# Threshold attention and a SoLU layer on one core: turning the weights of four slots on TensorE, and earlier loads

## The chip, the core and the metric

The kernel runs on one core of a Trainium2 chip. The metric is the device time of one execution in microseconds; before the change it is 865.18 us, the median of three runs (863.53 to 865.64). The engines are TensorE (PE, with its weight loads PEld), VectorE (DVE), ScalarE (ACT), GpSimd (POOL) and the queue engine SyncE (SP), which issues most of the transfers. Each works through its own list of instructions in order and waits on semaphores of the others.

## What is computed

Eight batches, eight heads, 576 rows of 64 per head: attention in which only scores within tau of the row's largest count, then a layer on the 4608 rows of 512 that result.

```python
scores = scale * np.matmul(q, k.transpose(0, 1, 3, 2))
thresh = np.max(scores, axis=-1, keepdims=True) - tau
scores = np.where(scores >= thresh, scores, -1000000000.0)
attn = np.exp(scores - np.max(scores, axis=-1, keepdims=True))
attn = attn / (np.sum(attn, axis=-1, keepdims=True) + 1e-09)
x = np.matmul(attn, v)                  # (B,H,S,D) -> rows of H*D = 512
h = x @ w_in                            # 512 x 1024
sm = softmax(h); solu = h * sm
ln = (solu - mu) / np.sqrt(var + 1e-06) * g_ln
out = ln @ w_out                        # 1024 x 512
```

All is float32; the two weight matrices and g_ln arrive as 64-bit numbers and are turned into float32 on the chip.

## The kernel before

**Slots and rounds.** The attention is cut into 144 slots, 18 to a batch. A slot is 128 score rows (64 rows twice) of a pair of heads, `(b, kind, hp, r)`: batch, half of the sequence, pair of heads, and first or second 128 rows. Slots 0 to 7 are the first half of batch 0, two for each of four pairs of heads. The main loop has a round for each slot, and the order of each engine's instructions is the order in which the loop writes them. In round s:

- `scores` (L472): TensorE multiplies q and k of slot s into two PSUM tiles `s_ps`, one per head, 576 columns each. If k and q of a later pair have to be turned, those products (L337) come first, into spare columns of the same tiles, and `keeps` copies them out (L374, L399, L415, L419).
- `maxes` (L494): VectorE reduces both tiles to the row's extreme and adds tau.
- `ramp` (L509) and `exps` (L518): ScalarE makes the threshold and the exponential, with the row's sum.
- `normalise(s - 1)` (L525 to L528): POOL inverts the sums of the slot before and scales its weights `w`, 576 columns for each head.
- `blocks(s - 1)` (L540, L549, L551): VectorE transposes them in 32 x 32 blocks into `T`; after the second slot of a pair SP issues three transfers that reorder the blocks into `wT`, 1.18 MB in all.
- `attend_steps` (L582) and `attended` (L614): three or four rounds after the pair's second slot TensorE multiplies v by `wT`, in 36 products of 128 columns (72 records in the trace), into a PSUM tile `pv`, and ScalarE copies the result to `xh`. The list `pv_due` holds the rounds: 5, 7, 9 and 10 for the pairs of slots 0 to 7.

**The layer.** When four pairs are in, `xh` holds two tiles of 128 rows. For each tile TensorE computes h in two rounds (`ff_h`, L647), then VectorE, ScalarE and POOL make maximum, exponential, product, statistics and normalisation (`ff_max` L662 to `ff_norm2` L718), a transfer swaps halves (`ff_swap` L729), VectorE transposes (`ff_turn` L739), and TensorE computes the output in two rounds (`ff_o`, L752). The first h stands in round 11, then 12, and 13 and 14 for the second tile; the first output stands in round 17.

**Weights.** The sixteen pieces of the two matrices are handled one a round in rounds 0 to 15: loaded four rounds ahead (`weight_load`, L270), taken apart by VectorE (L284, L287, L302) and ScalarE (L290), added by POOL (L312). The pieces of w_out are also multiplied by g_ln (L317) and copied to the other half of the partitions by two transfers (`weight_d`, L324). An output product may not start before the sixteenth piece.

**PSUM.** Four tiles of two banks: `s0` and `s1` for the scores, `p0` and `p1` (handed out by `take`) for everything else: turned heads, `pv`, `h_ps`, `o_ps`.

**Buffers.** `w` has four buffers (two slots), `wT` two, `u` and `V`, which the layer uses, one each.

**Loads.** `load_at` gives the round in which SP issues a load: v of batch 0 in rounds 0, 1, 3 and 5; k and q of batch 1 in rounds 10, 11, 15 and 16; its v in 17, 18, 24 and 25. SP issues in order too, and a transfer that waits for a buffer holds back those behind it.

Of the kernel before, what the change touches and what calls it, by code (L numbers as in the profile page):

```python
# [20 lines left out]
def kernel(  # L21
# [47 lines left out]
    ident = const.tile([P, P], F32, name="ident")  # L69
    swapped = const.tile([P, 64], F32, name="swapped")  # L70
    w1 = const.tile([P, NP, DFF], F32, name="w1")
# [147 lines left out]
    def constants():  # L219

        nc.gpsimd.memset(seed, 0.0)
        nc.scalar.activation(out=ntau, in_=seed, func=AF.Exp)
        make_identity(nc, ident)
        for g in range(2):
            of = 64 + 32 * (1 - g)
            nc.gpsimd.tensor_copy(
                out=swapped[ROWS[1], 32 * g : 32 * g + 32], in_=ident[ROWS[1], of : of + 32]
            )
        nc.gpsimd.memset(mhalf, -0.5)
        nc.gpsimd.memset(mone, -1.0)  # L230
        nc.gpsimd.memset(zero, 0.0)

        nc.vector.tensor_scalar(
            out=scl, in0=tau_t, scalar1=0.0, scalar2=SCALE, op0=ALU.is_ge, op1=ALU.mult
        )
        nc.vector.tensor_scalar(
            out=tau_t, in0=tau_t, scalar1=0.0, scalar2=104.0, op0=ALU.max, op1=ALU.min
        )  # L240
        nc.vector.tensor_scalar(out=ntau, in0=tau_t, scalar1=-1.0, scalar2=None, op0=ALU.mult)
# [89 lines left out]
    def turn(spare, x, lhsT_of, swap=False):  # L331

        o = spare["base"] + 64 * x
        to = slice(o, o + 64)
        for r in range(2):
            for y in range(2):
                nc.tensor.matmul(  # L337
                    out=spare[r][ROWS[y], to], lhsT=lhsT_of(r, y),
                    rhs=swapped[ROWS[1]] if swap and r else ident[ROWS[r], ROWS[r]],
                    start=True, stop=True,  # L340
                )
# [106 lines left out]
    live = {}  # L448

    def scores(s, items):  # L450
        b, kind, hp, r = slots[s]
# [9 lines left out]
        for ks in (slice(SM, S), slice(0, SM)):  # L461
            for h in range(2):
                for y in range(2):
                    if kind < 2:
                        d = pairs[b * NP + hp]
                        t = P * (2 * kind + r) if b < 2 else 32 * NK * r + P * kind
                        t += 64 * y
                        lhsT = d["qT"][ROWS[h], t : t + 64]
                    else:
                        d = pairs[b * NP + r + 2 * y]  # L470
                        lhsT = d["qe"][ROWS[h]]
                    nc.tensor.matmul(  # L472
                        out=ps[h][ROWS[y], ks], lhsT=lhsT, rhs=d["kT"][ROWS[h], ks],
                        start=True, stop=True,
                    )
# [31 lines left out]
    def ramp(s, x):  # L507
        d = live[s]
        nc.scalar.activation(  # L509
            out=d["w"][x], in_=d["w"][x] if d["loose"] else d["ps"][x][:, 0:S], func=AF.Prelu, bias=d["nth"][x], scale=-1.0,  # L510
            alpha=1.0e30,
        )
# [9 lines left out]
    def normalise(s):  # L522
        d = live[s]
        sm = d["sm"]
        nc.gpsimd.tensor_scalar(out=sm, in0=sm, scalar1=1e-9, scalar2=None, op0=ALU.add)  # L525
        nc.gpsimd.tensor_tensor(out=sm, in0=sm, in1=mone, op=ALU.pow)  # L526
        for x, w in enumerate(d["w"]):
            nc.gpsimd.tensor_scalar(  # L528
# [29 lines left out]


    def attend_steps(key):  # L560
        b, kind, hp = key
        unit = units[key]
        wT = unit["wT"]
        unit["y"] = take("pv")
        _, y = unit["y"]
        y = y.rearrange("p (u n) -> p u n", u=2)

        for e in range(2) if kind == 2 else [None]:
            for m in range(NK):
                for u in range(2):  # L570
                    d, h0 = source(b * NP + (hp if e is None else e + 2 * u))
                    for h in range(2):
                        if e is None:
                            how = "p (r g x) -> p g r x" if b < 2 else "p (g r x) -> p g r x"
                            to = y[ROWS[h], u, 0:P].rearrange(how, r=2, g=2)
                            rhs = wT[ROWS[u], :, m, :, h]
                        else:
                            to = y[ROWS[h], u, 64 * e : 64 * e + 64].rearrange(
                                "p (g x) -> p g x", g=2
# [11 lines left out]
                        yield  # L591

    def attended(key):
        b, kind, hp = key
        tag, y = units.pop(key)["y"]
        y = y.rearrange("p (u n) -> p u n", u=2)[:, :, 0:P]
# [10 lines left out]
        else:  # L607
            if hp == 0:
                xh[b, kind] = work.tile(
                    [P, NP, 256], F32, tag=f"xh{(2 * b + kind) % 4}", bufs=1, name="xh"  # L610
                )
            how = "p (r u y) -> p u r y" if b < 2 else "p (u g x r) -> p u g r x"
# [185 lines left out]
    for s, (b, kind, hp, r) in enumerate(slots):  # L798
        if r == 1:
            pv_due.append((s + LAG_PV + (s < 6 or s in (11, PER - 1, PER + 9)), (b, kind, hp)))  # L800
# [17 lines left out]
    for at, job, hf, what in (  # L818
        (11, load_one, 0, "q"),
        (10, load_one, 0, "k"),  # L820
        (15, load_one, 1, "k"),
        (16, load_one, 1, "q"),
        (17, load_v, 0, (0,)),
        (18, load_v, 0, (1, 2)),
        (PER + 6, load_v, 1, (0,)),
# [34 lines left out]
    with tc.manual_schedule():  # L860
# [16 lines left out]
        whole = {0: 1, 2: 2, 4: 3}  # L877
        for r, hf, parts in ((0, 0, (0,)), (1, 0, (1, 2)), (3, 1, (0,)), (5, 1, (1, 2))):
            load_at[r] = [lambda hf=hf, parts=parts: load_v(0, hf, parts)]

        ready = []
# [8 lines left out]
        while True:  # L890
# [10 lines left out]
            if rnd == NS:  # L901
# [8 lines left out]
                assert quarter != 3  # L910
            if rnd == 13:
                prev, cur, quarter = cur, None, 0
# [9 lines left out]
            if more:  # L922
# [18 lines left out]
                maxes(rnd, loose)  # L941
                ramp(rnd, 0)
                if rnd == 0:
                    weight_a(0)
                if not loose:
                    keeps(rnd, 0)
                    keeps(rnd, 1)
                ramp(rnd, 1)
                exps(rnd)
            if rnd in whole:  # L950
# [30 lines left out]
            elif step == ("h", 1):  # L981
                ff_h(cur, 1, None, beside)
                quarter = 2
                by = rnd + 2 * (rnd == 14)
                late.setdefault(by, []).append(lambda t=cur: (ff_max(t), ff_exp(t)))
# [9 lines left out]
                if cur == (0, 1, 1):  # L995
                    middle.setdefault(rnd + 6, []).append(lambda t=cur, at=rnd + 6: ff_turn(t, at))
                else:
                    late.setdefault(at, []).append(lambda t=cur, at=at: ff_turn(t, at))
                if not more:
# [15 lines left out]
            if attending is not None:  # L1015
# [6 lines left out]
                elif kind < 2 and hp == NP - 1:  # L1022
                    ready.append((rnd + 1, [(b, kind, 0), (b, kind, 1)]))
            if rnd - 1 in live:
                blocks(rnd - 1)
# [8 lines left out]
            if rnd == 3:  # L1034
                gains()
            if rnd in pieces:
                x = pieces[rnd]
                weight_b(x)
                for y in {0: (3, 4), 11: (), 12: (15,)}.get(x, (x + 4,)):
                    if y < len(pieces):  # L1040
                        weight_load(y)
                if x + 1 < len(pieces):
                    weight_a(x + 1)
            for job in load_at.pop(rnd, []):
# [39 lines left out]
```

## Time and profile before

| | |
|---|---|
| median of three runs | 865.18 us |
| the profiled execution | 864.95 us, its span 863.2 us |
| PE busy | 817.0 us (95%) |
| VectorE, ScalarE, POOL busy | 673.5, 572.1, 495.1 us |
| PE idle before 118.4 us, and after | 34.9 us, 11.3 us |
| granted TensorE clock, mean | 0.981 |

The rounds begin (start of the first L494, in us) at 35.14 (round 5), 40.37, 44.33, 49.25, 53.51 (round 9), 60.34, 70.05 (round 11), 74.46, 80.88, 85.95, 92.47 (round 15), 100.24, 105.19, 110.20 (round 18) and 118.40 (round 19).

The busy time of an engine is read stage by stage, since the first 118 us, in which the weights are prepared, go by other limits than the rest. A line of waits gives the waiting engine with tile and line, the releaser, the sum in us, how often, and the longest. A line of the chain gives a start, a length in us and what ran; a line of the timeline adds count and, in brackets, the idle time before it and who ended it.

### The profile page before, as it was taken

Reading aid. Unit: us, or ns where it says so; the run is one execution under the profiler, and the core shown is the slowest. Engines: PE = TensorE matmul, PEld = TensorE weight load, DVE = VectorE, ACT = ScalarE, POOL = GpSimd, SP = SyncE. Lnnn points to the kernel's source line nnn. Section 1 sums busy time; section 2 is a strip of 40 time slices with the busy share of each in tenths; the row PEclk is TensorE's granted clock in tenths of the full one; section 3 lists DMA queues with packets and bytes.
Section 4 is the critical chain, followed back from the end, with each engine's and each line's share of the span. In section 5 each row is a group of like instructions: output and inputs, shape, how many; then the busy total and the mean of one; then the engine's idle time right before and its main releaser. Section 6 shows DMA issues by size and latency. Waiting matters only on the chain.

```text
span 863.2 us, 36114 instructions
## 1 busy us (share of the span) xinstructions
PE 817.0 (95%) x15361; PEld 634.7 (74%) x15361; DVE 673.5 (78%) x1232; ACT 572.1 (66%) x1153; POOL 495.1 (57%) x936
## 2 busy tenths in 40 slices
PE   4659789999999999999999999999999999999997
PEld 3437567777688888888788886777788888887655
DVE  4987777978788888888788887888888888787361
ACT  5876867777667767777677766767677776775121
POOL 2876756566666656565656655565666655555120
PEclk9878999999999999999999999999999999999999
DMA  9999796997878778888788787888788887555312
GB/s 288 243 254 251 185 203 162 234 248 196 224 196 219 202 196 208 220 214 198 201 202 222 198 194 192 212 222 206 183 228 229 193 196 186 154 141 140 69 38 62
DMA packets 83712, 168.54 MB, mean 195 GB/s; under 512 B 15448, under 2 KB 45152, under 8 KB 83552
## 3 DMA queue, kind: packets, MB, share of 16 engines
q1 hardware_dynamic: 82416, 164.25, 75.5%
q8 instruction: 120, 1.97, 1.0%
q10 hardware_dynamic: 1136, 2.00, 0.7%
q14 instruction: 40, 0.33, 0.1%
HBM read 46.14 MB, written 9.44 MB: 64 GB/s over the span
## 4 chain that ended last, share of the span: by engine, by line
PE 84%; DMA 6%; ACT 4%; issue 2%; DVE 2%; POOL 1%; SPq 1%; ACTq 0%; DVEq 0%
PE o_ps L752 26%; PE h_ps L647 23%; PE s_ps L472 16%; PE pv L582 15%; DMA wT<-T 4%; PE h_ps L637 3%; ACT w L509 1%; ACT w L518 1%; DMA qT<-flip 1%; DMA w<-w 1%; DVE w L494 1%; DMA k<-in_k_dram 1%; ACT qT L374 0%; PE s_ps L337 0%; POOL w L528 0%
## 5 line engine op out<-in xcount | busy, mean ns | idle before, releaser
L752 PE MATMUL o_ps<-w,uT 64*64 64x256 f32 x4608 | 273.1, 376 | 4.3 <-issue 1.9
L494 DVE CUSTOM_DVE_ANT_0 w<-s_ps,tau_t 128x576 f32<-128x576 f32 x280 | 200.0, 751 | 94.4 <-PE s_ps L472 67.0
L509 ACT ACTIVATE w<-s_ps,nth 128x576 f32<-128x576 f32 x280 | 197.0, 739 | 110.8 <-DVE nth L494 90.8
L752 PEld LDWEIGHTS o_ps<-w,uT 64*64 64x64 f32 x4608 | 221.5, 133 | 59.3 <-ACT xh L614 12.0
L528 POOL TENSOR_SCALAR w<-w,sm 128x576 f32<-128x576 f32 x288 | 221.5, 781 | 14.3
L540 DVE STREAM_TRANSPOSE T<-w 128x576 f32<-128x576 f32 x288 | 207.5, 755 | 22.0 <-POOL w L528 20.6
L647 PE MATMUL h_ps<-w,xh 64*64 64x512 f32 x1856 | 223.1, 589 | 0.7 <-issue 0.7
L518 ACT ACTIVATE w<-w,ntau 128x576 f32<-128x576 f32 x288 | 219.8, 768 | 0.0
L582 PEld LDWEIGHTS pv<-wT,v 64*64 64x64 f32 x5760 | 179.7, 137 | 37.4 <-issue 12.8
L472 PE MATMUL s_ps<-kT,qT 64*64 64x512 f32 (+1 forms) x2048 | 177.1, 413 | 14.0 <-ACT w L509 12.0
L582 PE MATMUL pv<-wT,v 64*64 64x128 f32 (+1 forms) x5760 | 179.5, 266 | 9.7 <-DMA wT<-T 7.2
L647 PEld LDWEIGHTS h_ps<-w,xh 64*64 64x64 f32 x1856 | 131.7, 133 | 65.4 <-issue 10.6
L525 POOL TENSOR_SCALAR sm<-sm 128x2 f32<-128x2 f32 x144 | 34.7, 241 | 203.7 <-ACT w L518 200.1
L526 POOL TENSOR_TENSOR sm<-sm,mone 128x2 f32<-128x2 f32 x144 | 105.8, 735 | 12.0
L472 PEld LDWEIGHTS s_ps<-kT,qT 64*64 64x64 f32 x2048 | 76.0, 136 | 21.1 <-ACT w L509 16.4
L614 ACT COPY xh<-pv 128x256 f32<-128x256 f32 x64 | 25.0, 390 | 83.3 <-PE pv L582 83.2
L713 ACT ACTIVATE V<-u,nb,rs 128x1024 f32<-128x1024 f32 x36 | 44.7, 1241 | 39.6 <-POOL nb L703 32.6
L739 DVE STREAM_TRANSPOSE uT<-V 128x1024 f32<-128x1024 f32 x36 | 44.3, 1230 | 15.2 <-DMA V<-u 14.8
L518 ACT ACTIVATION_READ_ACCUMULATOR w<-w,ntau 128x1 f32 x288 | 55.9, 194 | 0.0
L677 DVE TENSOR_TENSOR u<-h_ps,u 128x1024 f32<-128x1024 f32 x36 | 42.8, 1189 | 9.7 <-ACT u L671 9.7
L718 DVE TENSOR_SCALAR u<-u,rs,nb 128x1024 f32<-128x1024 f32 x36 | 35.5, 987 | 17.2 <-ACT V L713 17.1
L662 DVE TENSOR_REDUCE hm<-h_ps 128x1 f32<-128x1024 f32 x36 | 43.0, 1193 | 6.0 <-PE h_ps L647 3.3
(88 smaller groups left out, 562.9 us busy)
## 6 DMA issues: line engine op xcount, KB each, us to landing
wT<-T SPq DMA_DIRECT2D x160, 288.0 KB, 6.2
wT<-T SPq DMA_DIRECT2D x64, 576.0 KB, 5.5
V<-u SPq DMA_DIRECT2D x144, 64.0 KB, 3.4
out_dram<-ob SPq DMA_DIRECT2D x71, 128.0 KB, 2.5
q<-in_q_dram SPq DMA_DIRECT2D x24, 288.0 KB, 6.1
qT<-flip SPq DMA_DIRECT2D x48, 144.0 KB, 3.8
k<-in_k_dram SPq DMA_DIRECT2D x24, 288.0 KB, 5.9
kT<-flip SPq DMA_DIRECT2D x48, 144.0 KB, 4.2
```

Of the source, the lines that this page charges most:

```text
L472: nc.tensor.matmul(out=ps[h][ROWS[y], ks], lhsT=lhsT, rhs=d["kT"][ROWS[h], ks], start=True, stop=True,)
L494: nc.vector.tensor_tensor_reduce(out=w, in0=ps[:, 0:S], in1=(zero if loose else tau_t).to_broadcast([P, S]), scale=1.0, scalar=BIG, op0=AL ...
L509: nc.scalar.activation(out=d["w"][x], in_=d["w"][x] if d["loose"] else d["ps"][x][:, 0:S], func=AF.Prelu, bias=d["nth"][x], scale=-1.0, al ...
L518: nc.scalar.activation(out=w, in_=w, func=AF.Exp, bias=ntau, scale=1.0, accum_out=sm[:, x : x + 1])
L526: nc.gpsimd.tensor_tensor(out=sm, in0=sm, in1=mone, op=ALU.pow)
L528: nc.gpsimd.tensor_scalar(out=w, in0=w, scalar1=sm[:, x : x + 1], scalar2=1.0, op0=ALU.mult, op1=ALU.mult)
L540: nc.vector.transpose(out=T[:, :, r, h, :], in_=w)
L582: nc.tensor.matmul(out=to, lhsT=d["v"][ROWS[u], (h0 + h - u) % 4 if b > 1 else h0 + h, m ^ 4 * u if m < 8 and b < 2 else m,], rhs=rhs, sta ...
L647: mm = nc.tensor.matmul(out=h[ROWS[y], f], lhsT=x[ROWS[r], c, ROWS[y]], rhs=w1_parts[ROWS[r], c, part ^ r], start=part == 0 and c == 0, st ...
L713: nc.scalar.activation(out=V, in_=u, func=AF.Identity, bias=nb, scale=rs)
L739: nc.vector.transpose(out=uT, in_=d["V"].rearrange("p y (m x) -> p m y x", x=32))
L752: nc.tensor.matmul(out=d["o"][ROWS[z], 512 * (r ^ other) : 512 * (r ^ other) + 256], lhsT=d["uT"][ROWS[r], m].rearrange("p y x -> p (y x)" ...
```

## The change

In slots 4 to 7 (`EARLY`) the weights are no longer scaled by POOL, transposed by VectorE and reordered by transfers. `ramp` writes them with the two halves of the columns interleaved. POOL makes two 64 x 64 diagonals of the inverted sums, `diag`, for each head (`ones` holds the unit matrices and their swapped forms, and replaces `swapped`), `turn_weights` multiplies the weights by the diagonals on TensorE, which turns and scales them at once, into two PSUM tiles, and VectorE copies them out to `wT`. `attend_early` multiplies v by them one slot at a time, a round later, and ScalarE copies each slot's 2 x 64 columns to `xh`. From round 5 to round 9 both free PSUM tiles are held for this (`front`), and the products of the pairs of slots 0 to 3 in rounds 5 and 7 go into the same tiles, and are now issued ahead of `exps`.

`xh` is complete in round 9, and the first tile's h stands in rounds 9 and 10, the second tile's still in 11 and 12, so that what follows from h comes two rounds sooner for both; `ff_turn` of the first stays in round 16 and the outputs stay where they were. v of batch 0 is loaded in rounds 0 to 3; k and q of batch 1 in rounds 6 to 9; the first half of its v in rounds 11 and 12. In rounds 5 to 8 the weight pieces are handled ahead of the turn.

```diff
-                    rhs=swapped[ROWS[1]] if swap and r else ident[ROWS[r], ROWS[r]],
+                    rhs=ones[ROWS[1], 0] if swap and r else ident[ROWS[r], ROWS[r]],
...
+    EARLY = range(4, 8)
+    front, turned_w = {}, {}
...
     def ramp(s, x):
         d = live[s]
+        to, of = d["w"][x], d["w"][x] if d["loose"] else d["ps"][x][:, 0:S]
+        if s in EARLY:
+            to = to.rearrange("p (m k c) -> p c m k", c=2, m=NK)
+            of = of.rearrange("p (c m k) -> p c m k", c=2, m=NK)
...
     def normalise(s):
...
+        if s in EARLY:
+            d["diag"] = diag = work.tile([P, 2, 64], F32, tag="uV"[s % 2], bufs=1, name="diag")
+            for x in range(2):
+                nc.gpsimd.tensor_scalar(
+                    out=diag[:, x], in0=ones[:, x], scalar1=sm[:, x : x + 1], scalar2=1.0,
+                    op0=ALU.mult, op1=ALU.mult,
+                )
+            return
...
+    def turn_weights(s):
+        d = live.pop(s)
+        pt = front["tiles"]
+        for m in range(NK):
+            for u in range(2):
+                for h, w in enumerate(d["w"]):
+                    nc.tensor.matmul(
+                        out=pt[u][ROWS[u ^ h], 64 * m : 64 * m + 64],
+                        lhsT=w[ROWS[u], 64 * m : 64 * m + 64], rhs=d["diag"][ROWS[u], h],
+                        start=True, stop=True,
+                    )
+        turned_w[s] = wT = work.tile([P, 2, S], F32, tag="wT", bufs=2, name="wT")
+        for u in range(2):
+            nc.vector.tensor_copy(out=wT[:, u], in_=pt[u][:, 0:S])
+
+    def attend_early(s):
+        b, kind, hp, r = slots[s]
+        wT = turned_w.pop(s)
+        pt = front["tiles"]
+        d, h0 = source(b * NP + hp)
+        for m in range(NK):
+            for v in range(2):
+                for h in range(2):
+                    nc.tensor.matmul(
+                        out=pt[v][ROWS[h], S : S + 64],
+                        lhsT=d["v"][ROWS[v], h0 + h, m ^ 4 * v if m < 8 else m],
+                        rhs=wT[ROWS[v], v ^ h, 64 * m : 64 * m + 64],
+                        start=m == 0, stop=m == NK - 1,
+                    )
+        for v in range(2):
+            of = P * r + 64 * v
+            nc.scalar.copy(out=xh[b, kind][:, hp, of : of + 64], in_=pt[v][:, S : S + 64])
...
-        (11, load_one, 0, "q"),
-        (10, load_one, 0, "k"),
-        (15, load_one, 1, "k"),
-        (16, load_one, 1, "q"),
-        (17, load_v, 0, (0,)),
-        (18, load_v, 0, (1, 2)),
+        (7, load_one, 0, "q"),
+        (6, load_one, 0, "k"),
+        (8, load_one, 1, "k"),
+        (9, load_one, 1, "q"),
+        (11, load_v, 0, (0,)),
+        (12, load_v, 0, (1, 2)),
...
-        for r, hf, parts in ((0, 0, (0,)), (1, 0, (1, 2)), (3, 1, (0,)), (5, 1, (1, 2))):
+        for r, hf, parts in ((0, 0, (0,)), (1, 0, (1, 2)), (2, 1, (0,)), (3, 1, (1, 2))):
...
+            if rnd == EARLY[0] + 1:
+                front["tags"], front["tiles"] = zip(take("pt"), take("pt"))
-            if rnd == 13:
+            if rnd == 11:
...
                 ramp(rnd, 0)
+                if rnd - 2 in EARLY:
+                    attend_early(rnd - 2)
+                    if rnd - 2 == EARLY[-1]:
+                        pairs_free.extend(front.pop("tags"))
+                        del front["tiles"]
+                    if rnd - 2 == EARLY[-2]:
+                        ready.append((rnd + 1, [(0, 0, 0), (0, 0, 1)]))
...
                 ramp(rnd, 1)
+                if "tiles" in front and pv_due[0][0] <= rnd:
+                    key = pv_due.pop(0)[1]
+                    for _ in attend_steps(key):
+                        pass
+                    attended(key)
                 exps(rnd)
...
-                by = rnd + 2 * (rnd == 14)
+                by = rnd + 2 * (rnd == 12)
...
+                    at = max(at, 16)
                     late.setdefault(at, []).append(lambda t=cur, at=at: ff_turn(t, at))
...
-            if rnd - 1 in live:
+            if rnd - 1 in EARLY:
+                weights_on(rnd)
+                turn_weights(rnd - 1)
+            elif rnd - 1 in live:
                 blocks(rnd - 1)
```

## The prediction

> **What bounds the kernel now.** The slices of the span come first, to see where TensorE idles:
>
> ```profile
> PE   4659789999999999999999999999999999999997
> ...
> PEclk9878999999999999999999999999999999999999
> DMA  9999796997878778888788787888788887555312
> ```
>
> TensorE is short of work in the first six slices (130 us) and full afterwards. Then the busy times by stage, cut where rounds begin (a round begins when VectorE starts its first L494; columns: stage, length, then busy time and count for PE, PEld, DVE, ACT, POOL, then clock, DMA share, GB/s):
>
> ```profile
> 35.10:53.50 18.40, 11.56 (x208) 7.49 (x208) 17.12 (x37) 15.57 (x35) 14.93 (x20) 0.87 1.05 241
> 53.50:70.10 16.60, 11.58 (x180) 9.50 (x184) 8.41 (x20) 8.72 (x19) 11.19 (x15) 0.63 1.02 268
> 70.10:92.50 22.40, 21.46 (x375) 14.71 (x371) 20.28 (x42) 19.05 (x42) 15.58 (x23) 1.00 0.92 221
> 92.50:118.40 25.90, 20.39 (x460) 14.48 (x455) 18.76 (x35) 20.14 (x46) 17.62 (x30) 0.93 0.84 204
> 118.40:863.20 744.80, 733.46 (x13778) 576.94 (x13769) 586.12 (x1050) 484.47 (x957) 418.25 (x816) 1.00 0.75 188
> ```
>
> These are rounds 5 to 8, 9 and 10, 11 to 14, 15 to 18, and the rest. Rounds 5 to 8 are VectorE's (17.12 of 18.40). In rounds 9 and 10 every engine is half idle. After 118.4 TensorE idles for 11.3 us in 744.8: what is won or lost earlier arrives at the end undiminished, so the sum only has to be made up to round 19. The waits of TensorE and the chain show what the idle time of rounds 9 and 10 is:
>
> ```profile
> PE s_ps L472 <- ACT w L509: 6.7, 6, 3.0
> PE pv L582 <- DMA wT<-T: 5.3, 4, 3.2
> PE o_ps L752 <- DMA w<-w: 1.8, 1, 1.8
> ```
>
> ```profile
> 52.72 0.60 SPq L551
> ...
> 53.37 11.33 DMA wT<-T
> ...
> 64.74 3.79 PE pv L582 x65
> ```
>
> ```profile
> 61.03 0.75 DVE L494 CUSTOM_DVE_ANT_0 w<-s_ps,tau_t 128x576 f32<-128x576 f32 x1
> ...
> 70.05 0.76 DVE L494 CUSTOM_DVE_ANT_0 w<-s_ps,tau_t 128x576 f32<-128x576 f32 x1 [5.66 <-PE s_ps L472]
> ```
>
> The weights of slots 6 and 7 are reordered by a transfer that lands 11.33 us after its issue, because the DMA engines are full (share 1.02). The product behind it (L582) then runs at half clock, and the scores of the next round stand behind both in TensorE's queue.
>
> **The change part by part.** Times are of the profiled execution (span 863.2, itself 864.95, 0.23 below the median 865.18). Up to round 5 little differs: four more POOL copies of 0.19 each at 1.4 us, while TensorE waits for k until 5.89; v's second half is issued one to two rounds sooner, and its reader is later still. So round 5 starts at 35.14 as now.
>
> *Rounds 5 to 8, one slot turned in each.* VectorE loses two transposes (0.71 each) and gains two copies of 576 columns out of PSUM. No such copy is in the trace; bounds are 0.67 (the 256-column L399 copy, 0.34 per step, scaled) and 0.76 (L494, 576 columns out of PSUM); I take 0.71: no change. POOL loses two L528 (0.74 each), gains two 64-column products, between 0.24 (L525) and 0.74; either is done before it is needed. ScalarE's copies shrink to 0.10 (64 columns, the step of L419) and 0.15. The ramps of these slots write every second element; bounds are nothing and the 6% by which L614's copies that write so (399 ns in the middle of the run against 378 early) are longer, 0.04 each; I take 0.02, nothing. TensorE gains 36 turning products of 64 columns per slot: 72 records at 1.04 (L582's 64-column group in round 21) to 1.5 (L337's 32 records in about 0.65): I take 1.2. The attention of a slot is 1.04, against 2.0 for a pair at full clock.
>
> What counts is the order. In the changed program the third turning product, whose operands its predecessors already had, waits for ScalarE again: the turned weights and the attention results share the pair of PSUM tiles, so a turn waits for the copies to xh, which stand in ScalarE's queue behind the first ramp. VectorE's copies wait for the turn, and the next L494 stands behind them. Round 6 is then: half of L494 0.68, semaphore 0.15, ramp 0.63, two copies 0.2, turn 0.1 + 1.2, drain 0.2, VectorE 1.42: 4.5 against 3.96 now. Round 8 the same: 4.55 against 4.26. In rounds 5 and 7 a pair's product goes ahead of the turn, and exps waits for it too. Round 5: L582 ends at 39.1 as now, then 0.55 to ScalarE's copies done, turn 1.3, drain 0.2, copies 1.42: 7.45 against 5.23. Round 7: 1.6 to the xh copies as in round 6, product 2.0, 0.55, turn 1.3, 0.2, 1.42: 7.2 against 4.92. Sum +2.2 + 0.5 + 2.3 + 0.3 = **+5.3**. Bounds: +3.5 (turn 1.04, copies 0.67, hand-overs half as long) and +12.5 (half clock, below).
>
> *Rounds 9 and 10.* No transfer is waited for: slots 4 to 7 need none. Round 9: 1.6 to the xh copies, h of 3.4, scores 0.7, 0.1: 5.8 against 6.83. Round 10: 0.3, h 3.4, 0.15, L662 1.15, then L302 to L287 1.25: 6.25 against 9.71 (round 12 now has this content and lasts 6.42). **-4.5.** Bounds -5.5 and -2 (the pair of slots 8 and 9 is late, below).
>
> *Rounds 11 to 14.* Softmax, statistics and normalisation of the first two tiles come two rounds sooner. VectorE sets rounds 11 and 12: 1.36 + 1.42 + 1.11 + 1.25 = 5.1, and 5.5 with L692's 1.45 in place of 1.11. In 13 and 14 TensorE has only scores and turned q and k, ScalarE has V (1.14), which waits for POOL's nb, and the second exp (1.1): 5.0 and 5.4. Together 21.0 to 22.3 as the clock goes; I take 21.6 against 22.4: **-0.8**.
>
> *Round 15* now lasts 7.8: V waits for nb, and scores with the turns take 3.5 at half clock. V has gone to round 13. ScalarE: 1.4 late from round 14, ramps 1.27, keeps 1.15, then TensorE 1.95 at full clock or 3.5: 5.6 to 7.2, middle 6.4: **-1.4**.
>
> *Rounds 16 and 17* get the second tile's statistics and V in place of exp and product: **+0.3**.
>
> *Round 18* (8.2) holds the 1.8 wait for L324's last weights, issued at 107.93 behind q (512 KB) and ahead of v. Both leave the queue here for rounds 6 to 12, and ScalarE's exp no longer precedes L317. The wait goes, and the idle TensorE behind it: **-2.2**, bounds 0 and -3.2.
>
> SP's moved issues: k and q in rounds 6 to 9 find free buffers (last read by round 4); six wT transfers of 2.36 MB are gone from rounds 6 to 8, so about 0.6 MB per round comes and 1.2 per two rounds goes. Behind these loads in the queue stand the weight loads, which have four rounds, and from round 9 L324, which is not read before round 17.
>
> Sum: 5.3 - 4.5 - 0.8 - 1.4 + 0.3 - 2.2 = **-3.3**; 864.95 - 3.3 = **861.6**.
>
> The clock is the rule that speaks against this. The rows: 0.63 in rounds 9 and 10, after a TensorE wait of 3.25; 1.00 in rounds 11 to 14, which h kept busy. [...]
>
> **The rivals.**
> - *Half clock in rounds 13 to 15.* TensorE has 2 us of work in each of rounds 13 and 14, and the same work in round 15 now shows half clock. Each costs up to 1.6 (3.5 against 1.95), less what VectorE hides: 0.6, 1.3, 0.8 above the forecast: **864.3**. Against it: the pair product of round 15 and the q and k turns. Chance 0.20.
> - *Transfers are waited for anyway.* The pair of slots 8 and 9 has two rounds from issue to product, as slots 6 and 7 have now, and 11.33 to landing would be 2.5 too long: **864.1**. Against: its rounds lose 2.36 MB. Chance 0.08.
> - *Slower: half clock in rounds 5 to 8.* Each turn then costs 1.0 more, each attention 0.45 on the path, the product of round 7 1.45: 4.0 + 1.8 + 1.4 = 7.2: **868.8**. It decides against the change once 6.2 of these 7.2 are paid. For it: clock 0.87 there and full half-clock stretches at 36 to 38.5. Against: TensorE's idle gaps shrink to about 1 us. Chance 0.15.
> - *More is won.* The hand-overs in rounds 5 to 8 are shorter (-1.8), round 15 runs at full clock (-0.8), round 18 gives 3.2: -3.6 on the forecast: **858.0**. Chance 0.20.
>
> **How the numbers follow.** The forecast keeps 0.37, nine tenths of it beyond 0.3% (2.6 us, about what a measurement of this kernel can tell). Faster: 0.20 + 0.33 = 0.53; same: 0.04 + 0.20 + 0.08 = 0.32; slower 0.15. The range 857.5 to 867.5 leaves out most of the slower case and the end of the better one; the forecast's own is 859.5 to 863.
>
> **What would show it.** Rounds 5 and 7 above 7 us with VectorE idle ahead of its PSUM copies; no wait for wT in rounds 9 and 10 and clock 1.00 there; round 11 starting within 1.5 us of 70.05; rounds 15 and 18 shorter by 1 to 2 each; the stretch behind round 19 still 744 to 746. It is wrong if rounds 5 to 8 take over 26 us, if a product waits for wT in round 12, or if the stretch behind 19 changes length.

## The result

The changed kernel takes 876.71 us (median of four runs, 876.15 to 878.96) against 865.41 (863.53 to 870.28) for the kernel before beside it: a ratio of 1.0127, 95% interval 1.0081 to 1.0172. It is slower by 1.3%; 861.6 was forecast, with a range up to 867.5. The profiled execution has a span of 874.6 us against 863.2.

The slices of the span of the changed kernel:

```profile
PE   5669599989989999999999999999999999999997
...
PEclk9989799999999999999999999999999999999999
DMA  8977865898868778887788888887788777655312
```

TensorE is again full only after some 130 us. By stage (columns as before; the cuts are the starts of rounds 5, 9, 11, 15, 16 and 19):

```profile
35.20:65.90 30.70, 21.02 (x714) 15.83 (x714) 17.47 (x38) 17.09 (x43) 10.89 (x21) 0.89 0.80 218
65.90:78.80 12.90, 12.51 (x189) 5.38 (x193) 10.25 (x20) 8.97 (x19) 9.23 (x14) 1.00 0.52 142
78.80:101.70 22.90, 16.35 (x286) 9.48 (x282) 21.20 (x43) 18.45 (x40) 18.98 (x28) 0.81 0.94 223
101.70:111.25 9.55, 6.50 (x144) 5.21 (x140) 4.50 (x8) 7.19 (x16) 4.40 (x8) 0.68 0.76 190
111.25:128.00 16.75, 15.17 (x322) 10.90 (x318) 13.84 (x27) 13.11 (x31) 10.89 (x20) 0.94 0.61 140
128.00:874.60 746.60, 734.00 (x13786) 569.14 (x13778) 584.27 (x1049) 484.33 (x957) 418.53 (x816) 1.00 0.74 187
```

Rounds 5 to 8 have grown from 18.4 to 30.7 us, and now no engine fills them: VectorE still has 17.5 us of work there, as before, but it has lost its place as the bound.

| us | before | forecast | after |
|---|---|---|---|
| rounds 5, 6, 7, 8 | 5.23, 3.96, 4.92, 4.26 | 7.45, 4.5, 7.2, 4.55 | 5.98, **11.07**, 8.85, 4.79 |
| rounds 9, 10 | 6.83, 9.71 | 5.8, 6.25 | 6.66, 6.26 |
| rounds 11 to 14 | 22.4 | 21.6 | 22.9 |
| round 15 | 7.8 | 6.4 | **9.5** |
| rounds 16 and 17 | 10.0 | 10.3 | 10.1 |
| round 18 | 8.2 | 6.0 | 6.7 |
| the rest | 744.8 | 744.8 | 746.6 |

The places to explain are rounds 6 and 7, and round 15. The waits of TensorE up to 120 us name an unusual releaser:

```profile
PE pt L603 <- issue: 5.3, 2, 4.9
PE pt L586 <- issue: 1.1, 1, 1.1
```

"issue" is time in which an engine waits for nothing that the profile shows. The timeline of TensorE has the places:

```profile
38.46 1.30 PE L586 MATMUL pt<-diag,w 64*64 64x64 f32 x70 [0.26 <-ACT xh L662]
...
41.32 1.04 PE L603 MATMUL pt<-wT,v 64*64 64x64 f32 x55 [0.34 <-DVE wT L593]
47.26 0.70 PE L603 MATMUL pt<-wT,v 64*64 64x64 f32 x15 [4.91 <-issue]
48.34 2.21 PE L586 MATMUL pt<-diag,w 64*64 64x64 f32 x72 [0.38 <-ACT xh L611]
...
58.49 1.16 PE L586 MATMUL pt<-diag,w 64*64 64x64 f32 x65 [1.14 <-issue]
```

In the middle of the product of slot 4 with its v, with all operands there, TensorE stops for 4.91 us; the turn of slot 5 behind it then takes 2.21 us where that of slot 4 took 1.30, at half clock (granted 0.50 from 45.0 to 51.8 us). VectorE's copy of the turned weights, and the next L501 behind that copy, wait for both.

What TensorE lacked, by the counts that follow, is its own instructions. They come on a queue of their own, in packets of 16.4 KB (1.97 MB in 120). Its line in the profile of the kernel before (packets, MB, share of the engines):

```profile
q8 instruction: 120, 1.97, 1.0%
```

And of the changed kernel:

```profile
q8 instruction: 124, 2.03, 1.0%
```

Of PE and PEld together the profile counts 30,722 records before and 31,586 after: about 256 for each packet. Counted through the trace, the stops of the changed kernel come after 1205, 1461 and 1713 records: 256 and 252 apart. That is about one packet's worth of records, which is called a page from here on. The packet for the long one started at 44.49 us and landed at 45.76; TensorE went on at 47.26. The page before had been begun at 38.8, so if the packet was asked for then, it stood 5.7 us before it started. Around it the DMA engines were full (length, engines, clock, DMA share, GB/s):

```profile
38.80:41.20 2.40, 2.18 (x86) 1.30 (x77) 1.36 (x3) 1.80 (x5) 0.93 (x2) 1.00 1.12 256
41.20:44.40 3.20, 1.04 (x55) 0.91 (x56) 3.09 (x8) 0.79 (x1) 1.84 (x3) 1.00 1.04 215
44.40:47.30 2.90, 0.04 (x4) 0.03 (x4) 0.00 (x0) 0.00 (x0) 0.00 (x0) 0.61 0.99 299
47.30:52.30 5.00, 4.62 (x116) 3.39 (x119) 1.47 (x3) 3.06 (x8) 1.54 (x5) 0.55 0.91 282
```

From 44.4 to 47.3 no engine does anything. In the kernel before, the packet of the same number was there by 43.5 and was needed at 55.6, and no stop shows in rounds 5 to 8. (The kernel before has one such stop all the same, 0.94 us at 91.1 us, in round 14: its trace already held the sign.) With the 36 turning products and the 36 more of each slot's own attention, rounds 5 to 8 use 5.6 pages (1428 records of PE and PEld) where the kernel before uses 1.6 (416), and with the DMA share at 1.04 the page that was needed at 42.35 us landed only at 45.76.

Round 15 is another matter. Its part of the chain:

```profile
92.85 0.88 SPq L176
...
94.18 6.41 DMA v<-in_v_dram
...
100.61 2.41 DMA V<-u
...
103.09 1.21 ACT u L736 x2
```

The exponential of the second tile (L736) waits for the first tile's swap of V and u, whose transfers stand in SP's queue behind the second batch's v, loaded now in rounds 11 and 12. Ramps, copies of q and k, and with them the next scores, stand behind that exponential in ScalarE's queue.

### The profile page after: what moved, and what is told of

Its sections match the earlier page's. It is cut to its first block, busy times and chain, and to the rows that moved or that the text cites. A ratio compares the mean times of both kernels' runs of the same rounds, so it can differ in the third digit from the quotient of the medians.

```text
span 874.6 us, 36985 instructions
## 1 busy us (share of the span) xinstructions
PE 826.6 (95%) x15793; PEld 629.2 (72%) x15793; DVE 674.2 (77%) x1232; ACT 573.3 (66%) x1161; POOL 491.0 (56%) x940
## 4 chain that ended last, share of the span: by engine, by line
PE 82%; DMA 5%; ACT 4%; SPq 3%; issue 3%; DVE 2%; POOL 0%; ACTq 0%; DVEq 0%
PE o_ps L817 26%; PE h_ps L712 22%; PE s_ps L479 15%; PE pv L638 14%; PE h_ps L702 3%; DMA wT<-T 3%; ACT w L520 1%; ACT w L528 1%; DMA v<-in_v_dram 1%; SPq L569 1%; PE pt L603 1%; SPq L794 1%; DVE w L501 1%; DMA k<-in_k_dram 1%; DMA w<-w 1%
## 5 line engine op out<-in xcount | busy, mean ns | idle before, releaser
L501 DVE CUSTOM_DVE_ANT_0 w<-s_ps,tau_t 128x576 f32<-128x576 f32 x280 | 200.2, 751 | 94.1 <-PE s_ps L479 63.5
L520 ACT ACTIVATE w<-s_ps,nth 128x576 f32<-128x576 f32 x280 | 197.8, 741 | 113.3 <-DVE nth L501 100.4
L817 PEld LDWEIGHTS o_ps<-w,uT 64*64 64x64 f32 x4608 | 223.8, 134 | 57.1 <-ACT xh L679 10.5
L546 POOL TENSOR_SCALAR w<-w,sm 128x576 f32<-128x576 f32 x280 | 215.4, 781 | 13.9
L558 DVE STREAM_TRANSPOSE T<-w 128x576 f32<-128x576 f32 x280 | 201.7, 755 | 19.7 <-POOL w L546 19.7
L638 PEld LDWEIGHTS pv<-wT,v 64*64 64x64 f32 x5472 | 165.3, 135 | 30.6 <-issue 9.1
L479 PE MATMUL s_ps<-kT,qT 64*64 64x64 f32 (+1 forms) x2048 | 179.7, 420 | 5.8 <-ACT w L520 4.6
L712 PEld LDWEIGHTS h_ps<-w,xh 64*64 64x64 f32 x1856 | 121.9, 133 | 73.9 <-issue 21.8
L638 PE MATMUL pv<-wT,v 64*64 64x128 f32 (+1 forms) x5472 | 164.6, 261 | 4.9 <-DMA wT<-T 1.8
L804 DVE STREAM_TRANSPOSE uT<-V 128x1024 f32<-128x1024 f32 x36 | 44.3, 1229 | 17.3 <-DMA V<-u 15.7
L736 ACT ACTIVATE u<-h_ps,hm 128x1024 f32<-128x1024 f32 x36 | 40.1, 1114 | 11.4 <-DMA V<-u 8.5
## 6 DMA issues: line engine op xcount, KB each, us to landing
out_dram<-ob SPq DMA_DIRECT2D x71, 128.0 KB, 2.5
```

The lines of the kernel that those rows point to most:

```text
L479: nc.tensor.matmul(out=ps[h][to, ks], lhsT=lhsT, rhs=d["kT"][ROWS[h], ks], start=True, stop=True,)
L501: nc.vector.tensor_tensor_reduce(out=w, in0=ps[:, 0:S], in1=(zero if loose else tau_t).to_broadcast([P, S]), scale=1.0, scalar=BIG, op0=AL ...
L520: nc.scalar.activation(out=to, in_=of, func=AF.Prelu, bias=d["nth"][x], scale=-1.0, alpha=1.0e30)
L546: nc.gpsimd.tensor_scalar(out=w, in0=w, scalar1=sm[:, x : x + 1], scalar2=1.0, op0=ALU.mult, op1=ALU.mult)
L558: nc.vector.transpose(out=T[:, :, r, h, :], in_=w)
L638: nc.tensor.matmul(out=to, lhsT=d["v"][ROWS[u], (h0 + h - u) % 4 if b > 1 else h0 + h, m ^ 4 * u if m < 8 and b < 2 else m,], rhs=rhs, sta ...
```

## The experiments

The theories: **F** (fetch): packets of TensorE's instructions come late behind full DMA engines, and TensorE's added records make it need them sooner. **C** (chain): the new hand-overs between TensorE, ScalarE and VectorE alone. **L**: the moved loads. Later **Q** (the packet is late whatever else moves) and, for round 15, **V** (the v load) against **K** (k and q, or the chain). All measured times are in one table; "issue" is the sum of such waits of TensorE in rounds 5 to 8 of the profiled execution, with the longest.

| kernel | median us | ratio to before (interval) | rounds 5 to 8 | issue (longest) | 9, 10 | 15 | 18 | 19 begins |
|---|---|---|---|---|---|---|---|---|
| before | 865.41 | | 18.4 | 0 | 16.5 | 7.8 | 8.2 | 118.4 |
| after | 876.71 | 1.0127 (1.0081 to 1.0172) | 30.7 | 6.5 (4.9) | 12.9 | 9.5 | 6.7 | 128.0 |
| a1 loads back | 874.65 | 1.0123 (1.0064 to 1.0183) | 28.7 | 4.7 (4.7) | 12.9 | 6.6 | 11.8 | 129.2 |
| a2 no raw | 872.65 | 1.0111 (1.0052 to 1.0169) | 30.2 | 5.0 (5.0) | 13.5 | 9.3 | 7.0 | 128.6 |
| a3 pairs | 875.62 | 1.0132 (1.0077 to 1.0187) | 28.8 | 5.4 (4.2) | 13.7 | 8.4 | 6.6 | 126.1 |
| b1 more products | 869.55 | 1.0101 (1.0063 to 1.0140) | 31.2 | 9.9 (6.0) | 12.6 | 7.5 | 10.5 | 130.0 |
| c1 light | 872.84 | 1.0140 (1.0091 to 1.0188) | 28.8 | 3.2 (3.2) | 12.9 | 6.9 | 11.1 | 128.6 |
| c2 loads only | 866.03 | 1.0053 (1.0025 to 1.0081) | 21.1 | 0 | 17.3 | 7.7 | 6.8 | 120.4 |
| c3 two slots | 879.75 | 1.0221 (1.0167 to 1.0275) | 34.0 | 4.6 (3.4) | 12.7 | 8.1 | 6.4 | 130.0 |
| c4 phase | 873.52 | 1.0132 (1.0068 to 1.0195) | 28.8 | 4.8 (2.6) | 13.9 | 9.2 | 6.3 | 130.7 |
| d1 no weights | 870.91 | 1.0103 (1.0070 to 1.0135) | 25.9 | 2.1 (2.1) | 13.5 | 7.9 | 6.9 | 122.8 |
| d2 late v | 875.47 | 1.0160 (1.0120 to 1.0200) | 31.0 | 3.9 (2.1) | 13.2 | 5.7 | 10.7 | 128.5 |
| d3 both | 872.73 | 1.0116 (1.0061 to 1.0171) | 27.2 | 2.8 (2.6) | 13.5 | 5.2 | 11.2 | 125.4 |
| d4 before, no weights | 862.18 | 0.9993 (0.9968 to 1.0019) | 18.4 | 0 | 12.1 | 7.3 | 8.1 | 115.1 |

The kernel before beside a and b had a median of 862.7, beside c 862.81, beside d 861.67. The stretch behind round 19 varies between 740.8 and 747.5 us among these profiles, with the same instructions in it, so single totals don't tell 3 us apart; rounds do.

**a1 loads back.** The second batch's k, q and v where the kernel before loads them:

```diff
-        (7, load_one, 0, "q"),
-        (6, load_one, 0, "k"),
...
+        (11, load_one, 0, "q"),
+        (10, load_one, 0, "k"),
```

> The changed kernel with k, q and v of batch 1 loaded in the old rounds (10, 11, 15 to 18), all else as in the change. Theory F (fetch): TensorE's own instructions come in packets on queue q8 (124 of them for 31,586 records, so 255 records each), and the 4.91, 0.41 and 1.14 us that rounds 6 and 7 lose to 'issue' lie 256 records apart: a burst of small products uses up a packet before the next has come through the full DMA engines. F expects little here, since the packet of the 4.91 was asked for before the first of these loads was issued: round 6 still above 9 us, rounds 5 to 8 above 28, total 873 to 876. Theory L (loads): the moved loads crowd the DMA engines and cost the time: rounds 5 to 8 back to about 24, round 15 below 8, total 863 to 867. Both expect the late exponential of round 14 (behind a load of v and the swap of halves) to be gone, for about 2 us.

**a2 no raw.** Part of the weights is not loaded:

```diff
+        if x in range(8, 12):
+            raws[x] = dict(raw=raws[x - 4]["raw"])
+            return
```

> The changed kernel without the loads of weight pieces 8 to 11 (2 MB, issued in rounds 4 to 7); the four pieces are made from the bytes of pieces 4 to 7 instead, so that part of w_out is left out of the computation. No instruction of TensorE, VectorE, ScalarE or POOL changes. Theory F: the DMA engines have room in rounds 5 to 7, q8's packets come through sooner, the 'issue' time of TensorE in rounds 6 and 7 falls from 6.5 to under 3, rounds 5 to 8 from 30.7 to 24 to 27, total 867 to 871. Theory C (chain: the hand-overs between TensorE, ScalarE and VectorE cost the time, by order alone): rounds 5 to 8 stay within 1 us of 30.7, total 875 to 878.

Neither shortens the long wait (4.7 and 5.0 us). L falls for rounds 5 to 8: with the loads of the second batch back in their places the stop is there. Only its round 15, below 8 us, came out (6.6), and round 18 took that back (11.8). F had expected a1's rounds 5 to 8 (28.7, above 28), but not a2's (30.2, where it had 24 to 27); there C's 30.7 within 1 us is met, though not its total. The trace has a reason: in both the DMA share stays about 1 from 35 to 47 us (0.97 to 1.20 in a1, 1.01 to 1.18 in a2). a1 still has the three weight pieces that SP issues from 38.7 on; in a2, with these gone, k, q and the ends of both, 1.3 MB, moved up into that time. Taking one load away did not empty the engines.

**a3 pairs.** Slots 4 and 5, and 6 and 7, multiplied with v as pairs, in rounds 8 and 9:

```diff
-                    attend_early(rnd - 2)
+                    if rnd in (8, 9):
+                        attend_early({8: 5, 9: 7}[rnd])
```

> The changed kernel with the attention of slots 4 and 5 in one group of 36 products of 128 columns in round 8, and that of 6 and 7 in one in round 9, instead of 36 of 64 columns in each of rounds 6 to 9: 144 records of products and 144 of weight loads fewer, 1.1 packets, and none of them in round 6. Theory F: the 4.91 of round 6 moves out to the turn of round 7 or goes; 'issue' in rounds 5 to 8 under 4, rounds 5 to 8 at 24 to 27, total 867 to 872. Theory C: one hand-over per round less in rounds 6 and 7, one more product of 2 us in 8 and 9: rounds 5 to 8 at 28 to 30, total 873 to 877.

The product in which TensorE stopped is gone from that place, and the stop is at the same count (1205) in the turn of slot 5 instead, 4.16 us. That is still in round 6, where F had it move to round 7 or go. Fewer records, but the same page to wait for: the times are C's numbers (28.8 and 875.62), the count is F's.

**b1 more products.** The kernel before, with nothing of the change but 72 products of the identity in each of rounds 5 to 8:

```diff
+            if rnd in range(5, 9):
+                tag, dm = take("dm")
+                for x in range(72):
+                    u, m = x % 2, x // 4 % 8
+                    nc.tensor.matmul(
...
+                pairs_free.append(tag)
```

> The kernel before, with 72 more products of 64 columns in each of rounds 5 to 8, of the unit matrix with itself into a free PSUM tile that nobody reads: TensorE's instruction count of the change without its chain of hand-overs. The work is 2.1 us a round at full clock, of which TensorE's idle time in rounds 5 to 8 (0.7, 2.0, 1.9 and 2.3 us) covers most. Theory F: TensorE loses 4 us or more to 'issue' in rounds 5 to 8, where before shows none, and the total rises by 3 to 9 us. Theory C: no hand-over, no loss: 'issue' below 1, total up by 0.5 to 2.

Products that wait for nothing and that nobody waits for make the kernel before slower by 1.0%. Its timeline of TensorE:

```profile
40.36 0.22 PE L472 MATMUL s_ps<-kT,qT 64*64 64x64 f32 x1
46.60 2.19 PE L472 MATMUL s_ps<-kT,qT 64*64 64x64 f32 x14 [6.02 <-issue]
...
54.29 2.21 PE L1028 MATMUL dm<-ident 64*64 64x64 f32 x137
59.59 0.28 PE L1028 MATMUL dm<-ident 64*64 64x64 f32 x3 [3.10 <-issue]
```

The two longest stops come after 1207 and 1975 records, three pages apart, one in score products and one in the added ones. C, which has no place for them, falls as the whole story. (This profile is of the longest of its ten executions, span 877.5; with a median of 869.55 the waits may be shorter in most.)

**c4 phase.** The changed kernel with 32 products of the identity (128 records, half a page) in round 2, as a direct test of the count:

```diff
+            if rnd == 2:
+                tag, dm = take("dm")
+                for x in range(32):
...
             if rnd == 3:
                 gains()
```

> The changed kernel with 32 products of 64 columns of the identity added in round 2 (128 records, half a page of 256; nothing reads them). Theory F: all page borders fall 128 records earlier in the program: the long issue wait leaves the product of slot 4 with its v, where it came after 57 of 72 matmul records, and stands in the score products of slot 6 instead, 14 records ahead of that product, with 4 to 6 us; total 873 to 880. If the wait came of what these instructions are or wait for, it would stay in the product of slot 4.

```profile
43.67 0.65 PE L479 MATMUL s_ps<-kT,qT 64*64 64x64 f32 x7
45.52 0.66 PE L479 MATMUL s_ps<-kT,qT 64*64 64x512 f32 x4 [1.20 <-issue]
...
46.06 1.59 PE L603 MATMUL pt<-wT,v 64*64 64x64 f32 x70
48.44 0.94 PE L586 MATMUL pt<-diag,w 64*64 64x64 f32 x48 [0.78 <-ACT xh L611]
52.00 0.91 PE L586 MATMUL pt<-diag,w 64*64 64x64 f32 x22 [2.63 <-issue]
```

The product of slot 4 (L603) now runs through without a stop. The stop stands where F put it, in slot 6's scores, after 1205 records, and the next after 1459 in the turn of slot 5. The place is settled: it goes with the count, not with the instruction. The size was wrong: 1.20 and 2.63 in place of 4 to 6, since the two packets started 2.0 and 3.9 us after the pages before them had been begun, in place of 5.7.

**c1 light and d1 no weights.** If the packets are late because the engines are full, emptying them must shorten the wait step by step. c1 is a1 and a2 together; d1 leaves out the weight pieces 4 to 11 (`range(4, 12)` in the edit of a2), whose first ones are issued at 27.7 us, and keeps the loads early.

> The changed kernel with both of the lighter settings at once: weight pieces 8 to 11 are not loaded (the bytes of pieces 4 to 7 stand for them, so part of w_out is left out of the computation) and the second batch's k, q and v are loaded in the rounds of the kernel before. Taken one at a time neither emptied the DMA engines between 36 and 48 us, as the next transfer in the queue moved up. Theory F (TensorE's instructions are fetched in packets, and a packet asked for while the DMA engines are full comes too late): the packet that was 5.5 to 5.8 us late starts within 2.5 us, the longest issue wait of TensorE in rounds 5 to 8 is under 2 us, and these rounds take 22 to 25.5 us in place of 30.7. Theory C (the new chain of hand-overs alone): 28 us or more, as in the changed kernel. Theory Q (the fetch is late whatever else moves): issue wait again 4 to 5.5 us. Round 15 short (6.5 to 7) as with the late loads alone, round 18 long (10 to 12), so the total is 864 to 871.

> The changed kernel without the loads of weight pieces 4 to 11 (the bytes of pieces 0 to 3 stand for them: half of the weights is left out of the computation); the second batch's loads stay early. Without the loads of pieces 8 to 11 and of the second batch the late packet still started only at 44.6 us, when the last transfers issued before 38 us were through; here 1.0 MB of those, issued at 27.7 and 29.5 us, is gone too. Theory F: that packet starts within 2.5 us of its request, no issue wait over 1.5 us in rounds 5 to 8, clock 0.9 or more in rounds 6 and 7, these rounds 22 to 25 us; total 865 to 870. Theory C: rounds 5 to 8 stay at 28 us or more, total 872 or more. Theory Q (late whatever else moves): issue wait 3 us or more.

Waits of TensorE in c1, rounds 5 to 8:

```profile
PE pt L606 <- issue: 3.2, 1, 3.2
```

The timeline of TensorE in d1:

```profile
41.30 1.04 PE L606 MATMUL pt<-wT,v 64*64 64x64 f32 x55 [0.34 <-DVE wT L596]
44.40 0.70 PE L606 MATMUL pt<-wT,v 64*64 64x64 f32 x15 [2.06 <-issue]
45.48 2.21 PE L589 MATMUL pt<-diag,w 64*64 64x64 f32 x72 [0.38 <-ACT xh L614]
...
49.25 1.27 PE L606 MATMUL pt<-wT,v 64*64 64x64 f32 x70 [0.34 <-DVE wT L596]
```

The wait at this page is 4.9 us with all loads, 3.2 with c1's, 2.1 with d1's; the packet starts 5.7, 4.3 and 3.2 us after the page before it is begun. That is the direction of F, but none of F's bounds was met: a wait over 1.5 us is left in d1, 25.9 is above 25, 870.91 above 870, and c1's 28.8 is C's number (28 or more), which falls in d1. Nor do three profiles prove a step each. d2, further down, has the same program and the same loads as the changed kernel up to round 10, and its wait at this page is the shortest:

```profile
45.32 0.46 PE L603 MATMUL pt<-wT,v 64*64 64x64 f32 x15 [1.38 <-issue]
```

The next packet is the better measure, since right behind a stop the start of a page is known. Behind this stop, at the same place in the program, it started 2.97 us later in the changed kernel and 4.70 in d2, with a DMA share of 1.04 and 1.02 until then, but 2.13 to 2.15 us later in a1, a2, c1, d1 and d3, with 0.00 to 0.68. Of all 24 stops of over 0.3 us in rounds 5 to 9, the ten with a share up to 0.68 behind them have the next packet after 1.1 to 2.2 us, and the fourteen with 0.86 or more after 2.8 to 5.4, one (1.7, in b1) excepted. So full engines do delay the packets, and Q falls; 1.1 to 2.2 us of the delay remain with a share up to 0.68.

Why the rest is so long stays open. In c1 SP issues nothing between 37.4 and 58.7 us, and still the packet starts only at 44.56, as the reordering transfers of slots 2 and 3 (issued up to 37.4) run out. That looks like waiting until what stands before it is done; but in the changed kernel two of these transfers landed at 45.45 and 47.02, after the packet had started. No run here shows what it waits for.

**c2 loads only.** The kernel before with the change's loads (the inverse of a1, and v of the first batch in rounds 2 and 3 in place of 3 and 5).

> The kernel before with nothing but the change's new places of the loads (first batch's second v in rounds 2 and 3, second batch's k, q, v in rounds 6 to 9, 11 and 12); no turn on TensorE. Theory F: TensorE's stream is as thin as before, so fuller DMA engines alone make no issue wait over 1 us in rounds 5 to 8, which take 18 to 21 us; total 860 to 868. Theory L (the moved loads themselves cost the time, by contention with the turned weights): rounds 5 to 10 take 5 us or more longer than before's 34.9, total 869 or more.

No stop in rounds 5 to 8, as F says: engines with a share of 0.99 to 1.18 from 35 to 52 us did no harm where the page was not needed soon. The loads are not free, though: 866.03, 0.5% slower. Rounds 5 to 10 take 38.4 us against 34.9, less than L's 5 us more. Of the 3.5 us, 2.8 stand in rounds 5 to 8 (21.1, just above F's 21), where round 7 alone is 3.1 longer. The rest is in 9 and 10, where one pair product now waits 7.3 us for the reordered weights behind these loads (waits from 53 to 75 us):

```profile
PE pv L582 <- DMA wT<-T: 7.6, 2, 7.3
```

Round 18 gets its 1.4 us back, which is less.

**c3 two slots.** `EARLY = range(6, 8)`: half of the change, with the pair of slots 4 and 5 by transfers and its product in round 8.

> The changed kernel with slots 6 and 7 alone turned by TensorE; slots 4 and 5 go by VectorE and DMA as before, and their product stands in round 8, so that h still begins in round 9. Theory F: half of the added records, so the page borders are reached later; longest issue wait in rounds 5 to 8 under 3.5 us, rounds 5 to 8 take 20 to 25 us; rounds 9 and 10 12.5 to 14; total 862 to 870. Theory C: half of the chain's cost, about 24.5 us for rounds 5 to 8 with issue waits unchanged at 4 to 5, total 868 to 872.

Worse than the whole (34.0 us in rounds 5 to 8): the waits for the reordered weights come back in round 7, and the page stop comes in round 8. Its timeline of TensorE:

```profile
46.82 0.69 PE L638 MATMUL pt<-wT,v 64*64 64x128 f32 x4 [2.71 <-DMA wT<-T]
...
60.49 3.69 PE L638 MATMUL pt<-wT,v 64*64 64x128 f32 x63 [3.41 <-issue]
```

Neither theory's times fit, only F's bound on the longest wait (3.4, under 3.5). Which of the two kinds of waits costs what was not taken apart.

**d2 late v, d3 both, d4 before without weights.** d2 puts the second batch's v in rounds 15 and 16 (k and q stay early); d3 is d1 with that; d4 is the kernel before with d1's edit, as footing.

```diff
-        (11, load_v, 0, (0,)),
-        (12, load_v, 0, (1, 2)),
+        (15, load_v, 0, (0,)),
+        (16, load_v, 0, (1, 2)),
```

> The changed kernel with the second batch's v loaded in rounds 15 and 16 in place of 11 and 12, k and q left early. Theory V (the swap of V and u stands behind the v load on SP's queue, the exponential of the second tile waits for it, scores for that): round 15 takes 6.3 to 7.2 us in place of 9.5, round 18 at most 8.5, total 872 to 875. Theory K (it is the k and q loads, or the chain ahead): round 15 stays above 8.5 us, total 876 and more.

> Both edits: no loads of weight pieces 4 to 11 (half of the weights left out), second batch's v in rounds 15 and 16. If F and V hold, the change is left with what the prediction's sum had: rounds 5 to 8 22 to 25 us, rounds 9 and 10 12.5 to 13.5, round 15 6.3 to 7.2, round 18 under 8.5, so the loose round 19 begins at 117 to 121 us; total 861 to 867. If C holds 866 to 872.

> The kernel before without the loads of weight pieces 4 to 11 (half of the weights left out), the footing for the two kernels above. It has no issue wait to lose, so rounds 5 to 8 take 17 to 19 us by F and by C alike; the waits of the pair products for the turned weights in rounds 9 and 10 shrink with the shorter queue, 16.5 to 12 to 15.5 us; total 857 to 863.

V holds: round 15 falls from 9.5 to 5.7 (below the expected 6.3), K falls. But round 18 rises from 6.7 to 10.7, over V's 8.5. SP's queue in d2 has the reason:

```profile
115.71 2.00 SPq L176 DMA_DIRECT2D v<-in_v_dram  x2
117.75 1.29 SPq L181 DMA_DIRECT2D v<-in_v_dram  x2
119.14 1.98 SPq L327 DMA_DIRECT2D w<-w  x2
```

And so have TensorE's waits in d2 from 110 us on:

```profile
PE o_ps L817 <- DMA w<-w: 3.0, 1, 3.0
```

Now the last weights' move (L327) stands behind v, and an output product waits for it, which in the kernel before cost 1.8. Rounds 15 and 18 together: 16.0 us before, 16.3 after, 16.3 in d2, 16.4 in d3. At both places tried the v load costs one of the two rounds, and no changed kernel has both of them shorter than before; the costs are not always equal, though: without the weight loads it is 14.7 with v early (d1). d3 missed its total (872.73 for 861 to 867) in two places: 27.2 us in rounds 5 to 8, where at most 25 was expected, and 11.2 in round 18 for under 8.5. d4 is as fast as before in its total, with rounds 9 and 10 at 12.1 us as expected: where the queue is short there is little waiting to save. Against it d1 is 8.7 us slower, 7.5 of it in rounds 5 to 8, so even leaving these loads out altogether doesn't bring the change below the kernel before, and postponing them can't be expected to. No run with the change beats the kernel before.

## Why the prediction was wrong

Working with the profiled executions: the forecast was -3.3 us, the spans say +11.4. Some of the prediction's sums are slightly off (the terms of round 6 give 4.58, of round 7 7.07, of round 15 5.77 to 7.32, and 0.34 scaled from 256 to 576 columns is 0.77, not 0.67), by too little to matter. The difference of 14.7 is 7.0 in rounds 5 to 8, 0.9 in 9 and 10, 1.3 in 11 to 14, 3.2 in round 15, -0.2 in 16 and 17, 0.7 in round 18, 1.8 behind round 19.

*Rounds 5 to 8, +5.3: the step that failed.* Every duration in it was near: the two PSUM copies take 0.71 each as taken, the turn 1.3 (1.2 taken), the ramps are 0.03 to 0.08 longer each (0.02 taken), round 8 came out near (4.79 for 4.55). Round 5 was shorter (5.98 for 7.45), at a clock of 1.00; in d2, the same program up to there, it took 7.48. What the sum did not have is TensorE's supply of instructions: "TensorE gains 36 turning products" was costed by their busy time alone. The stops at page borders took 6.5 us. Take the issue waits out of the length of these rounds, and the changed kernel has 24.2 us, a1 24.1, a2 25.1, a3 23.4, c1 25.6, c4 23.9, d1 23.8, d3 24.4 and d2 27.1, against the 23.7 forecast (18.4 + 5.3). So the chain of hand-overs was sized about right: C is right for its +5 and F for most of the rest. That 24.2 is so near is partly luck. Round 5 is 1.5 us shorter than forecast, and round 6 without its stop 1.7 longer, which is the half clock that follows the stop (0.9 in the turn of slot 5, 0.8 in the scores behind it); this is read from durations and was not tried by itself. d2 has the length of the changed kernel within 0.3 us with 3.9 us of stops, since its pair products of rounds 5 and 7 took 4.05 and 3.47 us, by their length mostly at half clock, where the changed kernel's took 2.40 and 2.30 at a clock of 1.00. That the waits are page stops is shown by their counts in eleven kernels, by c4, which moved them, and by b1, which made them in the kernel before; that full engines delay the packets, by the packets right behind a stop. No run has the change without any stop.

The rival "half clock in rounds 5 to 8" had the sign, and its condition came about (clock 0.61 and 0.55 at 44.4 to 52.3), but here as a consequence: the clock fell at 45.0, during the stop. Its 7.2 us were for every turn and product; only one turn and one set of scores paid. In d2 two pair products paid as well, the first of them ahead of any stop, so the rival was nearer than one profile shows. That TensorE's gaps would "shrink to about 1 us" was wrong for the one gap that mattered. The clock halved 2.7 us into the stop of 4.91, and in d1 1.9 us into one of 2.06.

*Rounds 9 and 10, -4.5 (measured -3.6).* Right in kind: no wait for wT, clock 1.00, round 10 6.26 for 6.25. Round 9 was 0.9 too short in the sum. d4 shows that this gain depends on the full queue: without the weight loads the kernel before has rounds 9 and 10 in 12.1 us.

*Rounds 11 to 14, -0.8 (measured +0.5).* Round 11 and 12 as worked out (5.1 and 5.3); 13 and 14 came out 0.6 and 1.4 longer, the first rival's 0.6 and 1.3, with a clock of 0.81 over the four rounds. That rival was the likelier case here.

*Round 15, -1.4 (measured +1.8): the second failed step.* "V has gone to round 13" was right, and so was the order on ScalarE; but the forecast followed behind the moved loads only the weight loads and L324. The swap of V and u stood behind the v load too, and the exponential waited 3.6 us for it. d2 shows it, and shows as well that with v at that later place the gain of round 18 (-2.2) is lost instead of that of round 15 (-1.4).

*Rounds 16 and 17, and 18.* +0.1 for +0.3, and -1.5 for -2.2, within its bounds; the wait for L324's weights was down to 0.5.

*Behind round 19.* 746.6 for 744 to 746, within what the same stretch varies between the other profiles.

## What to carry to other kernels

Count an engine's instructions as well as their time: here about every 256 records of TensorE took a packet of 16.4 KB, and bursts of small products placed where the DMA engines were full (a share of 0.91 to 1.12 around the changed kernel's longest stop) stopped at such borders, for up to 4.9 us there and 6.0 in b1, in whatever instruction stood there. The profile shows it as "issue" waits in the middle of a group whose operands are there; equal counts between them (here 256 and 252 records) tell it from a semaphore. And where a load moves in an in-order queue, list every transfer behind it at the new place, small ones too: a wait taken away in one round came back three rounds on (d2: round 15 from 9.5 to 5.7 us, round 18 from 6.7 to 10.7).

## What the runs showed of the hardware

- TensorE's instruction packets, 16.4 KB or about 256 records each, took 0.9 to 1.8 us to land in the kernel before and 0.9 to 1.7 in the changed kernel, and at stops of over 0.9 us TensorE went on 1.3 to 1.6 us after that. Right behind a stop in rounds 5 to 9 the next packet started 1.1 to 2.2 us later with a DMA share up to 0.68, and 2.8 to 5.4 with 0.86 or more, one of 1.7 excepted.
- The stops of over 0.9 us in rounds 5 to 8 fell at 177 to 183 records past a multiple of 256 in all eleven kernels that had them.
- 288 idle products in the kernel before, on an engine that was 63% busy in those rounds, cost 0.6 to 1.4% of the whole.
- The granted clock halved 1.9 us into a stop of 2.06 (d1) and 2.7 us into one of 4.91 (the changed kernel). In the changed kernel's profile it stood at half from 45.0 to 51.8 us, 92.8 to 103.0 and 106.5 to 113.3; in that of the kernel before, between 35 and 70 us, from 35.2 to 38.6, 52.2 to 59.0 and 62.5 to 69.3. In rounds 5 and 7 the same pair products took 2.40 and 2.30 us at a clock of 1.00 in the changed kernel's profile, and 4.05 and 3.47 us in d2's.
